# Moving operands of a router's small VectorE operations into PSUM, and an earlier turn of the last x

## The chip, the cores and the metric

The kernel runs on one NeuronCore of one Trainium2 chip. The metric is the device time of one execution in microseconds (us); lower is better. TensorE (PE) does the matrix products and transposes, VectorE (DVE) and ScalarE (ACT) elementwise work and reductions, GpSimd (POOL) elementwise work in SBUF and the indirect transfers, and SyncE (SP) issues most DMA transfers. TensorE writes its results to PSUM, which VectorE and ScalarE can read and write.

## The reference

A hashed attention (4 batches, 8 heads, 768 tokens, 64 wide) feeds a mixture of experts with one expert per token (3072 tokens, 512 wide, 8 experts, hidden width 1024). Cut to what matters:

```python
mask = q_bucket[:, :, :, None] == k_bucket[:, :, None, :]     # six sign bits of q @ proj
scores = np.where(mask, scale * (q @ k.T), -1e9)
attn = exp(scores - max) / (sum + 1e-9)
x = (attn @ v) laid out as (B * S, H * D)
logits = x @ w_gate + modality_bias[modality_id]
e_idx = argmax(logits); gate_w = softmax(logits)[e_idx]
out[e_idx == e] = gate_w * (relu(x @ w1[e]) @ w2[e])          # for each expert e
```

## The kernel before

Attention works on 16 pairs of heads, four pairs to a batch. TensorE's order in attention is written out by hand: for each pair the six strings of `PLAN`, one for each key tile (128 keys), name the steps to take (S: scores, M: the row maxima of the next pair, T: the transposes ("turns"), signs and patterns of the pair after it, A: the product with v, F, f, e, E: one step of `finish` of the batch before, x, y: two steps of `finish_x`, Q: the sum of denominators). A step is what a generator does up to its next `yield`. The other engines' orders are not written by hand: a scheduler fixes them at build time from its own model of the times, in the order of the trace unless an instruction's inputs come late. Each engine runs its queue in order.

GpSimd adds up the exponentials of each pair (L326, tile sp, 128x768, ten additions a pair); in the last pair VectorE takes half of them. `finish(b)` multiplies the gate weights with the unnormalised outputs (L376), turns the products (L385) and the denominators (L392), each copied from PSUM to SBUF by VectorE (L386, L393), inverts the denominators and forms the logits. `route(b)` then takes the best expert of each token, the softmax weight (L618 to L621) and, with a small matrix product of the one-hot choices (L613, L615), the token's place in its expert's list (L624 to L632); GpSimd writes (token, weight) to that place in a table in DRAM (L635). All of these are VectorE operations on 128 partitions by 2 to 104 elements, nearly all with inputs and outputs in SBUF. `finish_x(b)` turns the outputs back to rows (L424), scales them (L426) and writes x to DRAM (L428).

The experts work in blocks of up to 256 tokens of one expert; two early blocks ("e") take tokens of batches 0 to 2 alone, so that they can start while batch 3 is routed. `early_slots` and `late_slots` work out, from the counts per expert, which expert and which rows of the table belong to each block: `above` (L646, L648), `cumulate` (L653 to L657) and `assign` (L664 to L683). SyncE reads expert and row from that result, then loads the block's list (`tb`, L770) and the weights (`raw`, L752, L754, eight transfers of 512 KB per block); GpSimd gathers the rows of x (`xg`, L774). ScalarE casts each weight tile (L760) and VectorE or GpSimd forms its remainder (L762); the same is done to x (`xh`, `xl`, L787). TensorE then does three products for each tile (L797 to L799, L839 to L841).

Two PSUM buffers named `psx` serve the turns, signs, patterns, sums, `finish`, `route` and `finish_x`. In the last pair (i = 15) nothing is computed for a next pair. The early table is traced after attention:

```python
with tc.high_priority(offset=CFG["hpf"]):
    tabs["e"] = early_slots()
```

Of the kernel before, what the change touches and what calls it, by code (L numbers as in the profile page):

```python
# [74 lines left out]
def attention(ctx, actx, tc, a, x_d, l_d, route=None, setup=None):  # L75
# [292 lines left out]
    def finish(b):  # L368

        ts_ = [st[4 * b + c] for c in range(4)]  # L370
        gsb = bp.tile([P, S], F32, name="gsb")
# [19 lines left out]
        for j in range(3):
            nc.tensor.transpose(tp[:, j], gs[:, j * P:(j + 1) * P], ident)  # L392
        nc.vector.tensor_copy(out=gq.rearrange("p j h a c -> p (j h a c)"), in_=tp[:, 0:3].rearrange("p j r -> p (j r)"))  # L393
        yield
        gv = gn.rearrange("p t (h r) -> p t h r", r=16)
        f = bp.tile([P, NT, 8], F32, name="f")
        rin = bp.tile([P, NT, 8], F32, name="rin")
        rv = rin.rearrange("p t (c h) -> p t c h", h=2)
        for h in range(2):
            for half in range(2):  # L400
                ts = slice(3 * half, 3 * half + 3)
                nc.vector.tensor_scalar(out=rv[:, ts, :, h], in0=gq[:, 0:3, h, half, 0:4], scalar1=1e-9, scalar2=None, op0=ALU.add)
        yield
        nc.vector.tensor_scalar(out=f, in0=rin, scalar1=1e-8, scalar2=float(S), op0=ALU.is_lt, op1=ALU.mult)
        nc.vector.tensor_tensor(out=rin, in0=rin, in1=f, op=ALU.add)
        nc.vector.reciprocal(rin, rin)
        fin[b] = (ts_, rin)
        yield
        gl = bp.tile([P, NT, 8, 8], F32, name="gl")
        nc.vector.tensor_tensor(out=gl, in0=gv[:, :, :, 0:8], in1=rin.unsqueeze(3).broadcast_to([P, NT, 8, 8]), op=ALU.mult)  # L410
        yield
        lg = bp.tile([P, NT, 8], F32, name="lg")
        nc.vector.tensor_reduce(out=lg, in_=gl.rearrange("p t h e -> p t e h"), axis=AX.X, op=ALU.add)
        yield
        yield from route(b, lg, ps_x)
# [31 lines left out]
    with tc.manual_schedule(engines={mybir.EngineType.PE}):  # L447
# [19 lines left out]
        for i in range(NPR):  # L467
# [9 lines left out]
            for kt in range(NT):  # L477
                for c in PLAN[kt]:
# [44 lines left out]
E = 8  # L523
# [4 lines left out]
EARLY = CFG["early"]  # L528
NBIG, SURE_BIG = 13, 12 - EARLY
# [16 lines left out]
def router(ctx, tc, a, x_d, tab):  # L546
# [5 lines left out]
    step = const.tile([P, 2, 12], F32, name="kstep")  # L552
# [6 lines left out]
    run = [const.tile([P, E], F32, name=f"run{j}") for j in range(2)]  # L559

    def setup():
        for t, n in ((tok, "c_tok"), (e8, "c_e8"), (step, "c_step"), (slot, "c_slot"), (low, "c_low")):
            nc.sync.dma_start(out=t, in_=a[n])
        with tc.tile_pool(name="rtmp", bufs=1) as tmp:
# [24 lines left out]
            nc.gpsimd.memset(run[0], 0.0)  # L589

    scattered = []

    def route(b, lg, ps):
        l = wk.tile([P, NT, E], F32, name="l")
# [3 lines left out]
        d = wk.tile([P, NT, E], F32, name="rd")  # L598
        nc.vector.tensor_tensor(out=d, in0=l, in1=m.unsqueeze(2).broadcast_to([P, NT, E]), op=ALU.subtract)
        ex = wk.tile([P, NT, E], F32, name="rex")  # L600
        nc.scalar.activation(ex, d, AF.Exp)
        yield
        w = wk.tile([P, NT, E], F32, name="rw")
# [4 lines left out]
        nc.vector.tensor_tensor(out=oh, in0=w, in1=wm.unsqueeze(2).broadcast_to([P, NT, E]), op=ALU.is_equal)  # L608
        yield
        pp = ps.tile([P, HALF], F32, name="psx")  # L610
# [5 lines left out]
        rec = wk.tile([P, NT, 2], I32, name="rec", bufs=2)  # L616
        sm = wk.tile([P, NT], F32, name="rsum")
        nc.vector.tensor_reduce(out=sm, in_=ex, axis=AX.X, op=ALU.add)  # L618
        nc.vector.tensor_scalar(out=sm, in0=sm, scalar1=1e-9, scalar2=None, op0=ALU.add)
        nc.vector.reciprocal(rec[:, :, 1].bitcast(F32), sm)  # L620
        nc.vector.tensor_copy(out=rec[:, :, 0], in_=tok[:, b])  # L621
        yield
        rb = wk.tile([P, E], F32, name="rb")
        nc.vector.tensor_tensor(out=rb, in0=run[b % 2], in1=base, op=ALU.add)  # L624
        rk = wk.tile([P, NT, E], F32, name="rk")
        nc.vector.tensor_tensor(out=rk, in0=pp[:, 0:NT * E].rearrange("p (t e) -> p t e", e=E), in1=rb.unsqueeze(1).broadcast_to([P, NT, E]), op=ALU.add)
        nc.vector.tensor_tensor(out=run[(b + 1) % 2], in0=run[b % 2], in1=pp[:, 64:64 + E], op=ALU.add)
        nc.vector.tensor_tensor(out=rk, in0=rk, in1=oh, op=ALU.mult)
        pos = wk.tile([P, NT], F32, name="pos")
        nc.vector.tensor_reduce(out=pos, in_=rk, axis=AX.X, op=ALU.add)  # L630
# [3 lines left out]
        for t in range(NT):  # L634
            ins = nc.gpsimd.indirect_dma_start(out=tab, out_offset=bass.IndirectOffsetOnAxis(ap=posi[:, t:t + 1], axis=0), in_=rec[:, t], in_offset=None).ins  # L635
# [8 lines left out]
    def above(cnt, row, name):  # L644
        g = wk.tile([P, E, 12], F32, name="sg")
        nc.vector.tensor_tensor(out=g, in0=cnt.unsqueeze(2).broadcast_to([P, E, 12]), in1=step[:, row].unsqueeze(1).broadcast_to([P, E, 12]), op=ALU.is_gt)  # L646
        nb = wk.tile([P, E], F32, name=name)
        nc.vector.tensor_reduce(out=nb, in_=g, axis=AX.X, op=ALU.add)  # L648
        return nb

    def cumulate(nb, name):
        c2 = wk.tile([P, E, E], F32, name="sc2")
        nc.vector.tensor_tensor(out=c2, in0=low, in1=nb.unsqueeze(1).broadcast_to([P, E, E]), op=ALU.mult)  # L653
        cu = wk.tile([P, E], F32, name=name)
        nc.vector.tensor_reduce(out=cu, in_=c2, axis=AX.X, op=ALU.add)
# [332 lines left out]
```

## Time and profile before

| | us |
|---|---|
| median of 3 timed runs (864.04 to 867.50) | 866.99 |
| the profiled execution, its own time | 862.96 |
| its span in the profile | 861.1 |
| TensorE busy in the span | 801.3 |
| VectorE busy | 600.8 |
| ScalarE busy | 498.3 |
| GpSimd busy | 457.2 |

The profile is one execution; its times are counted from the start of the span. A row of the order in time says when a group began, how long it took from its first start to its last end, on which engine, at which line, what it wrote and read, how many instructions were merged, and in brackets how long the engine had been idle and what released it. [...]

### The profile page before, as it was taken

How to read it: one execution, taken by the hardware profiler on the slowest of the kernel's cores; microseconds unless marked ns; L12 is line 12 of the kernel's file. 1: busy time of each engine (PE TensorE's matmuls, PEld its weight loads, DVE VectorE, ACT ScalarE, POOL GpSimd, SP SyncE). 2: the span in 40 equal slices, each digit the busy share in tenths (PEclk: the TensorE clock that was granted, in tenths of full speed). 3: DMA queues.
4: the chain of work that ended last, by engine and by line, in shares of the span. 5: the costliest groups of instructions: out<-in, count | busy, mean ns of one | idle time of the engine just before them, and what ended most of it. 6: DMA issues, size and time to landing. Idle time of an engine off the chain costs nothing.

```text
span 861.1 us, 14524 instructions
## 1 busy us (share of the span) xinstructions
PE 801.3 (93%) x5154; PEld 590.9 (69%) x5154; DVE 600.8 (70%) x1029; ACT 498.3 (58%) x953; POOL 457.2 (53%) x347
## 2 busy tenths in 40 slices
PE   6799999999999999999989787889999999999993
PEld 3466666666667656566746345779999999998992
DVE  6777678797877897776877767766555565567650
ACT  4567676676667566566744343355555555557551
POOL 5377779677887867976667664232222221122110
PEclk9899999999999999999999797999999999999997
DMA  6423212320431132132101254597777767679650
GB/s 173 112 75 92 74 43 68 93 74 19 118 116 63 55 93 74 56 99 68 38 19 31 72 160 147 113 325 222 222 218 232 222 214 234 200 230 299 215 148 22
DMA packets 76753, 110.87 MB, mean 129 GB/s; under 512 B 10495, under 2 KB 52095, under 8 KB 76672
## 3 DMA queue, kind: packets, MB, share of 16 engines
q1 hardware_dynamic: 70880, 95.14, 37.4%
q0 software_dynamic: 4928, 13.14, 4.1%
q10 hardware_dynamic: 864, 1.57, 0.6%
q8 instruction: 43, 0.70, 0.3%
q14 instruction: 38, 0.31, 0.2%
HBM read 84.83 MB, written 13.33 MB: 114 GB/s over the span
## 4 chain that ended last, share of the span: by engine, by line
PE 75%; DVE 10%; issue 6%; DMA 4%; ACT 2%; POOL 1%; SPq 1%; POOLq 0%; DVEq 0%; ACTq 0%
PE psu L341 13%; PE pss L305 8%; PE pss L306 7%; PE psm L239 5%; PE yps L839 5%; PE yps L841 5%; PE yps L840 5%; PE hps L797 4%; PE hps L799 4%; PE hps L798 4%; PE psx L207 3%; PE psx L180 3%; PE psm L245 3%; PE psx L222 2%; PE psx L268 1%
## 5 line engine op out<-in xcount | busy, mean ns | idle before, releaser
L326 POOL TENSOR_TENSOR sp<-sp,pb 128x768 f32<-128x768 f32 x124 | 224.9, 1849 | 38.3 <-ACT pb L323 38.1
L762 DVE TENSOR_TENSOR w<-raw,w 128x1024 fp32r<-128x1024 f32 x108 | 138.9, 1287 | 99.6 <-ACT w L760 93.7
L241 DVE TENSOR_REDUCE mx<-psm 128x1 f32<-128x512 f32 x192 | 131.3, 687 | 41.6 <-PE psm L239 40.4
L760 ACT CAST w<-raw 128x1024 fp32r<-128x1024 f32 x112 | 116.9, 1047 | 69.7 <-PE yps L841 50.7
L341 PE MATMUL psu<-pb,vt 128*64 128x512 f32 (+1 forms) x768 | 137.4, 501 | 0.0
L318 ACT ACTIVATE pb<-pss 128x512 f32<-128x512 f32 x192 | 112.9, 609 | 27.1 <-PE pss L306 18.6
L797 PE MATMUL hps<-xh,w 128*128 128x256 f32 x384 | 109.4, 286 | 2.1 <-DVE hl L804 1.9
L798 PE MATMUL hps<-xl,w 128*128 128x256 f32 x384 | 109.1, 284 | 0.0
L799 PE MATMUL hps<-xh,w 128*128 128x256 f32 x384 | 108.8, 284 | 0.0
L341 PEld LDWEIGHTS psu<-pb,vt 128*64 128x64 f32 x768 | 51.8, 139 | 79.8 <-issue 73.1
L774 POOL DMA_INDIRECT xg<-x_d,tb x26 | 32.7, 1259 | 123.6 <-DMA tb<-tab 115.7
L847 POOL DMA_INDIRECT out<-y,tb x26 | 33.9, 1305 | 117.2 <-ACT y L846 63.9
L839 PE MATMUL yps<-w,hl 128*128 128x512 f32 x208 | 82.9, 398 | 0.9 <-DVE hl L827 0.9
L841 PE MATMUL yps<-w,hh 128*128 128x512 f32 x208 | 81.3, 391 | 0.0
L840 PE MATMUL yps<-w,hh 128*128 128x512 f32 x208 | 81.0, 389 | 0.0
L323 ACT ACTIVATE pb<-pss 128x512 f32<-128x512 f32 x96 | 57.7, 601 | 38.5 <-PE pss L306 36.0
L305 PE MATMUL pss<-m_0g,s_0g 128*128 128x512 f32 x192 | 71.5, 372 | 6.3 <-DVE m_0g L270 3.9
L797 PEld LDWEIGHTS hps<-xh,w 128*128 128x128 f32 x384 | 73.9, 193 | 3.5 <-DVE hl L804 2.6
L798 PEld LDWEIGHTS hps<-xl,w 128*128 128x128 f32 x384 | 73.9, 192 | 1.2 <-issue 0.8
L799 PEld LDWEIGHTS hps<-xh,w 128*128 128x128 f32 x384 | 73.8, 192 | 0.0
L803 ACT ACTIVATE hh<-hps 128x256 fp32r<-128x256 f32 x96 | 36.6, 384 | 64.0 <-PE hps L799 57.9
L305 PE MATMUL pss<-m_1g,s_1g 128*128 128x512 f32 x192 | 69.5, 362 | 1.2 <-ACT pb L323 0.8
(214 smaller groups left out, 1773.3 us busy)
## 6 DMA issues: line engine op xcount, KB each, us to landing
raw<-moe_w SPq DMA_DIRECT2D x112, 512.0 KB
qk<-q SPq DMA_DIRECT2D x32, 192.0 KB
qk<-k SPq DMA_DIRECT2D x32, 192.0 KB
vt<-v SPq DMA_DIRECT2D x16, 384.0 KB
x_d<-xs SPq DMA_DIRECT2D x18, 256.0 KB
m_1g<-m_1g SPq DMA_DIRECT2D x16, 192.0 KB
s_1g<-s_1g SPq DMA_DIRECT2D x16, 192.0 KB
m_0g<-m_0g SPq DMA_DIRECT2D x15, 192.0 KB
```

The costliest lines, as they stand in the source:

```text
L241: nc.vector.tensor_reduce(out=mx[:, qt + j, hi, 0:1], in_=mp, axis=AX.X, op=ALU.max)
L305: nc.tensor.matmul(out, t["s1"][h][:, ks], t["m1"][h][:, cs], start=True, stop=False)
L326: (nc.vector if h and i in CFG["spd"] else nc.gpsimd).tensor_tensor(out=t["sp"][:, h], in0=(t["pb"][0] if kt == 1 else t["sp"])[:, h], in1 ...
L341: nc.tensor.matmul(t["u"][part][64 * h:64 * h + 64, 0:w], t["v"][:, h, kt], t["pb"][kt][:, h, COLS[part]], start=False, stop=(kt == NT - 1 ...
L760: nc.scalar.copy(out=hi, in_=r)
L762: (nc.gpsimd if pool else nc.vector).tensor_tensor(out=lo, in0=r, in1=hi.bitcast(F32), op=ALU.subtract)
L797: nc.tensor.matmul(hps, lo[:, c, fs], xh[:, c], start=(c == 0), stop=False)
L798: nc.tensor.matmul(hps, hi[:, c, fs], xl[:, c], start=False, stop=False)
L799: nc.tensor.matmul(hps, hi[:, c, fs], xh[:, c], start=False, stop=(c == 3))
L839: nc.tensor.matmul(yps[g], hl[fc][:, gs], hi[:, fb], start=(fc == 0), stop=False)
L840: nc.tensor.matmul(yps[g], hh[fc][:, gs], lo[:, fb], start=False, stop=False)
L841: nc.tensor.matmul(yps[g], hh[fc][:, gs], hi[:, fb], start=False, stop=(fc == 7))
```

## The change

Small operations of `finish`, `route`, `early_slots` and, by form alone, `late_slots` are laid out anew. In `finish` the denominators are turned first and inverted from PSUM; the gate products are multiplied straight from PSUM, without the copies gn and gq; the logits and the operands that follow (l, d, w) lie in the unused half of the same psx tile, which `route` is handed. In `route` the places are worked out in the psx tile of the one-hot product, the constant 1e-9 is a ninth column of the exponentials, the running counts are kept a second time with the base added (runb), and the token numbers are written once at the start. `finish` has 13 steps instead of 19. `early_slots` gets a psx tile in which nearly every VectorE operation has one operand; two inputs that would both lie there are copied by ScalarE. It is traced inside attention, at the second key tile of the last pair. `late_slots` has the same code with an area in SBUF. Constants are folded so that `assign` has fewer operations. In the last pair, `finish_x` of batch 2 takes two steps at the start of each of the first three key tiles.

```diff
     def finish(b):
+        gs = gsum[b]
+        tp = ps_x.tile([P, MAIN], F32, name="psx")
+        for j in range(3):
+            nc.tensor.transpose(tp[:, j * P:(j + 1) * P], gs[:, j * P:(j + 1) * P], ident)
+        gq = tp[:, 0:3 * P].rearrange("p (j h a c) -> p j h a c", j=3, h=2, a=2)
+        r = tp[:, 3 * P:3 * P + 8 * NT].rearrange("p (t c) -> p t c", c=8)
...
+        nc.vector.tensor_scalar(out=f, in0=r, scalar1=1e-8, scalar2=float(S), op0=ALU.is_lt, op1=ALU.mult)
+        nc.vector.tensor_tensor(out=rin, in0=r, in1=f, op=ALU.add)
+        nc.vector.reciprocal(rin, rin)
+        yield
...
-            nc.vector.tensor_copy(out=gn[:, 4 * w:4 * w + n], in_=tp[:, 0:n])
...
-        nc.vector.tensor_copy(out=gq.rearrange("p j h a c -> p (j h a c)"), in_=tp[:, 0:3].rearrange("p j r -> p (j r)"))
...
+            nc.vector.tensor_tensor(out=gl[:, 4 * w:4 * w + n], in0=tp[:, 0:n * P].rearrange("p (t h r) -> p t h r", h=8, r=16)[:, :, :, 0:8],
+                                    in1=rin[:, 4 * w:4 * w + n].unsqueeze(3).broadcast_to([P, n, 8, 8]), op=ALU.mult)
+            if w == 0:
+                yield
+        area = tp[:, 2 * P:4 * P]
+        nc.vector.tensor_reduce(out=area[:, 0:48].rearrange("p (t e) -> p t e", e=8), in_=gl.rearrange("p t h e -> p t e h"), axis=AX.X, op=ALU.add)
+        yield from route(b, area, ps_x)
...
             for kt in range(NT):
+                if i == NPR - 1 and kt == 1:
+                    before_last(ps_x.tile([P, MAIN], F32, name="psx"))
+                if i == NPR - 1 and kt < 3:
+                    next(xs, None)
+                    next(xs, None)
...
-    def route(b, lg, ps):
+    def route(b, area, ps):
+        lg, l, d, w = (area[:, 48 * j:48 * j + 48].rearrange("p (t e) -> p t e", e=E) for j in range(4))
...
-        nc.vector.tensor_scalar(out=sm, in0=sm, scalar1=1e-9, scalar2=None, op0=ALU.add)
-        nc.vector.tensor_copy(out=rec[:, :, 0], in_=tok[:, b])
-        nc.vector.tensor_tensor(out=rb, in0=run[b % 2], in1=base, op=ALU.add)
...
+        rk, ro = (pp[:, 128 + 48 * j:176 + 48 * j].rearrange("p (t e) -> p t e", e=E) for j in range(2))
+        pos = pp[:, 256:256 + NT]
...
+    def above(cnt, row, sp, out):
+        cp = sp[:, 0:E]
+        nc.scalar.copy(out=cp, in_=cnt)
...
+        ns = wk.tile([P, E], F32, name="snb")
+        nc.scalar.copy(out=ns, in_=nb)
+        nc.vector.tensor_tensor(out=cx, in0=cu, in1=ns, op=ALU.subtract)
...
-        nc.vector.tensor_scalar(out=r, in0=r, scalar1=float(DUMMY), scalar2=None, op0=ALU.add)
-        nc.vector.tensor_copy(out=out[:, 1], in_=r)
+        nc.vector.tensor_scalar(out=out[:, 1], in0=r, scalar1=float(DUMMY), scalar2=None, op0=ALU.add)
...
+    return route, early_slots, late_slots, setup, lambda: wk.tile([P, 512], F32, name="area")
...
-        with tc.high_priority(offset=CFG["hpf"]):
-            tabs["e"] = early_slots()
+        tabs["e"] = eslot[0]
...
-        tabs["b"], tabs["s"], tot = late_slots()
+        tabs["b"], tabs["s"], tot = late_slots(late_area())
```

## Rows read from the trace of the kernel before

**Rows 1.** The page, engines' busy time, share of the span, instructions.

```profile
PE 801.3 (93%) x5154; PEld 590.9 (69%) x5154; DVE 600.8 (70%) x1029; ACT 498.3 (58%) x953; POOL 457.2 (53%) x347
```

**Rows 2.** Busy time by stretch (stretch, length, busy by engine, granted clock, DMA).

```profile
400.50:434.60 34.10, 30.90 (x210) 19.39 (x209) 28.59 (x59) 20.32 (x43) 25.47 (x19) 1.00 0.18 47
461.30:480.00 18.70, 15.23 (x86) 9.16 (x86) 16.06 (x44) 6.15 (x12) 16.75 (x15) 0.91 0.14 28
480.00:490.00 10.00, 5.84 (x31) 3.91 (x28) 9.47 (x6) 2.30 (x5) 7.41 (x5) 0.84 0.01 0
490.00:500.00 10.00, 7.87 (x34) 3.79 (x32) 2.91 (x4) 6.06 (x12) 2.25 (x1) 0.81 0.91 287
...
517.00:530.00 13.00, 6.74 (x35) 2.89 (x31) 9.91 (x7) 5.38 (x8) 8.54 (x6) 0.66 0.50 156
...
584.50:607.80 23.30, 23.30 (x154) 21.41 (x153) 14.04 (x19) 13.16 (x20) 5.35 (x4) 1.00 0.75 229
```

**Rows 3.** The chain that ended last, 475 to 500 us (start, length, what).

```profile
479.13 8.32 DVE selr L682
...
490.45 6.16 DMA raw<-moe_w
```

**Rows 4.** Order in time, VectorE and GpSimd, 459 to 488 us.

```profile
459.90 3.62 POOL L326 TENSOR_TENSOR sp<-pb,pb 128x768 f32<-128x768 f32 x2 [3.42 <-ACT pb L323]
460.97 0.21 DVE L626 TENSOR_TENSOR rk<-psx,rb 128x48 f32<-128x48 f32 x1
461.21 0.60 DVE L628 TENSOR_TENSOR rk<-rk,oh 128x48 f32<-128x48 f32 x1
463.04 0.50 DVE L632 CAST posi<-pos 128x6 int32<-128x6 f32 x1
473.22 14.19 POOL L326 TENSOR_TENSOR sp<-sp,pb 128x768 f32<-128x768 f32 x8
478.89 0.17 DVE L681 TENSOR_REDUCE selr<-selx 128x2 f32<-128x16 f32 x1
479.10 8.34 DVE L682 TENSOR_SCALAR selr<-selr 128x2 f32<-128x2 f32 x1
```

**Rows 5.** VectorE's groups by line, 100 to 480 us (busy us, mean ns, idle).

```profile
L293 DVE TENSOR_TENSOR vs<-psx,vs 32x64 fp32r<-32x64 f32 x24 | 5.4, 224 | 5.5 <-ACT vs L289 4.5 <-PE pss L306 0.9
L619 DVE TENSOR_SCALAR rsum<-rsum 128x6 f32<-128x6 f32 x3 | 5.3, 1773 | 0.1
L624 DVE TENSOR_TENSOR rb<-run,ke 128x8 f32<-128x8 f32 x3 | 4.6, 1526 | 0.0
L405 DVE TENSOR_TENSOR rin<-rin,f 128x48 f32<-128x48 f32 x3 | 0.6, 209 | 0.1
L626 DVE TENSOR_TENSOR rk<-psx,rb 128x48 f32<-128x48 f32 x3 | 0.6, 208 | 0.2
```

**Rows 6.** Order in time, TensorE, with what ended its waits.

```profile
433.62 0.50 PE L239 MATMUL psm<-s_0g,m_0g 128*128 128x512 f32 x1 [2.67 <-DVE mx L247]
468.17 0.51 PE L245 MATMUL psm<-s_1g,m_1g 128*128 128x256 f32 x2 [1.20 <-DVE mx L241]
488.10 0.55 PE L305 MATMUL pss<-m_0g,s_0g 128*128 128x256 f32 x1 [3.88 <-DVE m_0g L270]
```

**Rows 7.** Order in time, all engines, 505 to 530 us.

```profile
505.25 7.54 POOL L326 TENSOR_TENSOR sp<-sp,pb 128x768 f32<-128x768 f32 x3 [2.63 <-ACT pb L323]
...
517.77 0.99 POOL L774 DMA_INDIRECT xg<-x_d,tb  x1 [1.35 <-DMA x_d<-xs]
519.41 7.53 DVE L762 TENSOR_TENSOR w<-raw,w 128x1024 fp32r<-128x1024 f32 x2 [0.68 <-ACT w L760]
521.30 0.66 PE L785 MATMUL psx<-ident,xg 128*128 128x128 f32 x2 [3.19 <-DMA xg<-x_d,tb]
527.59 2.79 PE L376 MATMUL psx<-ut,gst 128*32 128x512 f32 x16 [2.38 <-DVE xl L787]
```

**Rows 8.** Tile psx, 185 to 225 us: ScalarE's evacuation (ns minimum/median/maximum).

```profile
L184 ACT CAST m_1g<-psx x4: 422/522/618, 188.5 to 218.1; 128x512 fp32r<-128x512 f32 x2, 128x256 fp32r<-128x256 f32 x2
```

More of the change, by code (lines that the diff above doesn't have):

```diff
@@ L398, in finish @@
[L398 to L415, printed above, removed]
+                nc.tensor.transpose(tp[:, j * P:(j + 1) * P], gsb[:, (4 * w + j) * P:(4 * w + j + 1) * P], ident)
@@ L528 @@
 EARLY = CFG["early"]
+NSTEP = N // TS
 NBIG, SURE_BIG = 13, 12 - EARLY
@@ L551, in router @@
     e8 = const.tile([P, 3, E], F32, name="ke8")
-    step = const.tile([P, 2, 12], F32, name="kstep")
+    step = const.tile([P, 2, NSTEP], F32, name="kstep")
     slot = const.tile([P, 16], F32, name="kslot")
@@ L559, in router @@
     run = [const.tile([P, E], F32, name=f"run{j}") for j in range(2)]
+    runb = [const.tile([P, E], F32, name=f"runb{j}") for j in range(2)]
+    rec = const.tile([P, B, NT, 2], I32, name="rec")
+    ex = const.tile([P, NT, E + 1], F32, name="rex")
+    wbase = const.tile([P, E], F32, name="wbase")
     def setup():
@@ L608, in route @@
         nc.vector.tensor_tensor(out=oh, in0=w, in1=wm.unsqueeze(2).broadcast_to([P, NT, E]), op=ALU.is_equal)
+        sm = wk.tile([P, NT], F32, name="rsum")
+        nc.vector.tensor_reduce(out=sm, in_=ex, axis=AX.X, op=ALU.add)
+        nc.vector.reciprocal(rec[:, b, :, 1].bitcast(F32), sm)
         yield
-        pp = ps.tile([P, HALF], F32, name="psx")
+        pp = ps.tile([P, 512], F32, name="psx")
         for j in range(NT):
@@ L683, in assign @@
[L683 to L694 removed]
+            w = cx
@@ new lines, in assign, with early_slots @@
+        nc.vector.tensor_scalar(out=out[:, 1], in0=r, scalar1=float(DUMMY), scalar2=None, op0=ALU.add)
+    def early_slots(sp):
+        out = const.tile([P, 2, EARLY], I32, name="eslot")
+        nb, cu, cx, r = (sp[:, 8 * j:8 * j + 8] for j in range(1, 5))
+        above(run[(B - 1) % 2], 0, sp, nb)
+        cumulate(nb, cu, cx)
+        es = wk.tile([P, E], F32, name="es")
+        nc.vector.tensor_scalar(out=es, in0=cx, scalar1=-1.0, scalar2=float(EARLY), op0=ALU.mult, op1=ALU.add)
+        nc.vector.scalar_tensor_tensor(out=early, in0=es, scalar=0.0, in1=nb, op0=ALU.max, op1=ALU.min)
+        assign(EARLY, cu, cx, wbase, TS, out, sp[:, 64:64 + EARLY * E], r[:, 0:EARLY])
@@ L701, in late_slots @@
         cnt = run[B % 2]
-        fb = above(cnt, 1, "fb")
-        nb = wk.tile([P, E], F32, name="lnb")
-        nc.vector.tensor_tensor(out=nb, in0=fb, in1=early, op=ALU.subtract)
-        cu, cx = cumulate(nb, "lcu")
-        assign(NBIG, cu, cx, early, TS, big)
-        sb = wk.tile([P, E], F32, name="sb")
-        nc.vector.scalar_tensor_tensor(out=sb, in0=fb, scalar=float(TS), in1=cnt, op0=ALU.mult, op1=ALU.is_lt)
-        su, sx = cumulate(sb, "lsu")
-        assign(NSML, su, sx, fb, 0, sml)
+        fbp, nb, cu, cx = (sp[:, 8 * j:8 * j + 8] for j in range(1, 5))
@@ L711, in late_slots @@
+        r = sp[:, 40:56]
+        above(cnt, 1, sp, fbp)
+        nc.vector.tensor_tensor(out=nb, in0=fbp, in1=early, op=ALU.subtract)
+        cumulate(nb, cu, cx)
         nc.vector.tensor_copy(out=tot[:, 0:1], in_=cu[:, E - 1:E])
-        nc.vector.tensor_copy(out=tot[:, 1:2], in_=su[:, E - 1:E])
         over = wk.tile([P, 2], F32, name="over")
         nc.vector.tensor_scalar(out=over[:, 0:1], in0=cu[:, E - 1:E], scalar1=SURE_BIG + 0.5, scalar2=None, op0=ALU.is_gt)
+        wb = wk.tile([P, E], F32, name="wb")
@@ new lines, in late_slots @@
+        eb = wk.tile([P, E], F32, name="eb")
+        nc.vector.scalar_tensor_tensor(out=eb, in0=early, scalar=float(TS), in1=wbase, op0=ALU.mult, op1=ALU.add)
+        nc.vector.scalar_tensor_tensor(out=wb, in0=fbp, scalar=float(TS), in1=wbase, op0=ALU.mult, op1=ALU.add)
+        assign(NBIG, cu, cx, eb, TS, big, sp[:, 128:128 + NBIG * E], r[:, 0:NBIG])
+        sb = sp[:, 64:72]
+        nc.vector.scalar_tensor_tensor(out=sb, in0=fbp, scalar=float(TS), in1=cnt, op0=ALU.mult, op1=ALU.is_lt)
+        su, sx = sp[:, 72:80], sp[:, 80:88]
```

116 lines of the change are left out of this document (44 added, 72 removed).

## The prediction

> **What bounds the kernel now.** I read the page first: TensorE is busy 93% of the span, VectorE 70% [rows 1]. A share says nothing of stages, so the busy time by stretch comes next [rows 2], each stretch a pair of heads or a step of the hand-over to the experts. The reader is to see two regimes. From 584.5 us on TensorE is full, 23.30 of 23.30 us for one block of 256 tokens, and stays so until the last blocks: whatever reaches that point earlier moves the end by as much. Before it lies the loss: 3.2 us idle in 400.5 to 434.6, 3.5 in 461.3 to 480, then 4.2 in 480 to 490, 2.1 in 490 to 500 and 6.3 in 517 to 530, with the granted clock at 0.91, 0.84, 0.81 and 0.66 in the last four. Then I read the chain of work that ended last, 479 to 498 us [rows 3]: it runs 8.32 us through one VectorE instruction at L682, goes to the slot loads, and then through a 6.16 us weight transfer.
>
> The order in time says why [rows 4]. L682 adds a constant to 128x2 values and takes 8.34 us. It starts inside GpSimd's run of eight denominator additions, 473.22 to 487.41, and ends as that run ends. At 461 us, inside another such run, L626 (one input in PSUM) takes 0.21 us and L628 (both in SBUF, same 128x48) 0.60; the conversion L632 (SBUF to SBUF) 0.50 for six values. Over the three routed batches the same split holds [rows 5]: L619 1773 ns and L624 1526, while L626 stays at 208 and L293, a PSUM input too, at 224. L405 (two SBUF inputs) shows the plain price, 209. So an elementwise VectorE instruction that lives wholly in SBUF waits for GpSimd; with an operand in PSUM it does not.
>
> **The change, term by term** (time on the path to 584.5).
>
> A, routing of batches 0 to 2. L619 and L624 lose their place, L608, L621, L628 and L632 get a PSUM operand or go. VectorE loses in waiting 3 x (1.77 - 0.17) + 3 x (1.53 - 0.17), about 9 us, with 0.17 us as the plain price of so small an operation (L681 [rows 4]), and some more at the others. Nearly all lies beside TensorE's own work: of TensorE's waits in these stretches only one follows a blocked chain, 2.67 us at 433.62 [rows 6], where the next maximum stood behind L619 and L621. I take 2.7 back; bounds 0 and 4.
>
> B, the table of early slots. Most of its operations ran ahead of maxima that pair 14 computes for pair 15; TensorE waited 1.20 us for one of these at 468.17 [rows 6]. They go to the last pair, which computes no maxima. 1.2; bounds 0 and the whole idle time of 461.3 to 480, 3.5.
>
> C, L682 itself. Its successor reads PSUM, so of 8.34 us about 0.16 remains: 8.2. Behind it on VectorE stood m_0g, for which TensorE waited 3.88 us [rows 6], and SyncE's load of the slot. The stretch 480 to 490 has no other owner. Bounds 4.2 (TensorE's own idle time there) and 8.3.
>
> D, the weight transfer in the chain [rows 3]. A cast that waits for its weights stands in ScalarE's queue ahead of the exponentials. The table came 8.2 us late to an order that was fixed at build time; in time, the wait should shrink. But the table is now traced at the second key tile of the last pair, and attention ends sooner, so some stays. TensorE's loss in 490 to 500 is 2.1 idle and 7.87 x 0.19 = 1.5 at the low clock. I take 2.0; bounds 0 and 6.2.
>
> F, the start of the experts. The last pair's x (three transposes, multiplies and SyncE writes) moves from its third, fifth and sixth key tile to its first three. SyncE's queue is moved past too: two of the writes should now stand before the weight loads, which follow the slot table. Before, the gather left at 517.77, released by x's last write, and landed after TensorE had waited 3.19 us [rows 7]. Those writes now land some ten us before attention ends. What then remains is the split of weights: two VectorE adds of L762 took 7.53 us beside GpSimd's own L762, and xl and TensorE's 2.38 us at 527.59 stand behind them [rows 7]. These adds are not changed. Of 517 to 530, 13 us, the work at full clock is 6.74 x 0.66 = 4.4, so 8.6 is lost; I take 4.0 for the gather, its idle time and a little clock; bounds 0 and 8.6.
>
> G, 530 to 584.5. The last batch's routing runs beside block 0; GpSimd does transfers there and a single weight split, so little was blocked. TensorE's small gaps stay. The late table keeps its operands in SBUF (its area comes from an SBUF pool) and gets three ScalarE copies, which hide behind blocks 0 and 1, since block 2 is the first to use it. If they don't, block 2's gather is late by a few us. 0; bounds -5 and 3.
>
> H, what is added. The logits, and the first steps of routing, live in one of the two psx buffers, so that turns, signs and x of the next steps have one; the early table (18 VectorE operations where there were 23, and two ScalarE copies, at most 0.5 us each by L184's [rows 8]) holds one for about 18 x 0.17 + 2 x 0.5 = 4.1 us. Two turns in a row then wait for an evacuation, 0.52 us [rows 8], once a batch and once in the last pair: -2.1. If four turns a batch wait 1 us each it is -12 and -4.1 more: bounds 0 and -16. Writing PSUM from VectorE is not in the trace: reading it costs nothing (L626 against L405), and the farthest row, L293, is 15 ns above; at most 26 instructions a batch make 0.4 us, off the path. That one I take as nothing. The copies into gn and gq that go lay beside TensorE's work: nothing, too.
>
> Sum: 2.7 + 1.2 + 8.2 + 2.0 + 4.0 - 2.1 = 16.0 us. The profiled execution took 862.96 us (span 861.1 and 1.9 around it); that gives 847. The three timed runs have a median of 866.99, 4.0 above the profiled one. The same gain from it gives **851 us**.
>
> [...]
>
> **Rivals.** (1) The forecast. (2) ScalarE's wait for weights stays: the casts stand before exponentials that are now sooner. For it speaks the 6.16 us in the chain; against it, that the lateness came from L682. D is not had, and one more such transfer is paid: 851 + 2 + 6 = 859.
>
> (3) Slower: the wait finds another instruction. L762 and the last pair's own L326 on VectorE still have two SBUF inputs. If the order now puts two weight splits into a long run of GpSimd in the last pair, VectorE stands for up to 14.2 us each (the run of eight [rows 4]), with m_0g, xs and the early table behind it. It decides from 20.3 us of such time (16.0 + 4.3); two full runs, 28.4 us, give 851 + 28 = 879. Against it: in the last pair VectorE takes half of the additions, and the longest run there was 7.54 us [rows 7].
> [...]
>
> (4) A PSUM operand, an output above all, puts a fixed term on each small operation. If it were a third of L405's 0.21 us, (3 x 26 + 18) x 0.07 = 6.7 us, half of it on the path, it gives 854. L626 speaks against it for inputs, nothing for outputs. [...]
>
> (5) The change does not do what it says: an output in PSUM does not free the instruction, and L682's successor waits as long. Then B, F and H remain, 3.1 us: 864. L626 and L293 speak against it, though both write SBUF.
>
> **How the numbers follow.** Chances: 0.62, 0.19, 0.08, 0.05, 0.06 in this order. The forecast's own range is 842 to 859: below, D and F at their full bounds (4.2 and 4.6 more); above, C at its lower bound, nothing of D and half of F (4.0, 2.0 and 2.0 less). The range for all is 839 to 864: at its low end A and B are had in full too (1.3 and 2.3), at its high end stands rival 5; left out above are rival 3 and the worst of H. About 0.5%, 4.3 us, is what a measurement of this kernel can tell from no change. Faster than 862.7: forecast, rivals 2 and 4, so 0.86. Rival 5 is the same, 0.06. Slower 0.08.
>
> **What would show it.** No VectorE instruction of the router or table above 0.4 us while GpSimd adds; the successor of L682 at 0.16 to 0.2 us; no TensorE gap of 2 us near L613 and the maxima (A, B); the last pair shorter by 8 us or more, with the granted clock near 1.0 (C); the gather's issue before the last additions of GpSimd (F); the first full stretch of TensorE starting near 568 us instead of 584.5. The prediction is wrong if ScalarE's cast waits again for weights inside the last pair (2), if L762 on VectorE is long there (3), if small PSUM operations take 0.27 us instead of 0.21 (4), or if turns wait for psx (H).

## The result and the profile after

The changed kernel takes 856.6 us (median of 4 runs, 854.1 to 860.46) where the kernel before takes 867.25 beside it: ratio 0.989, 95% interval 0.984 to 0.994, so 1.1% faster, inside the range and 5.6 us above the 851 forecast. Five more rounds gave 856.19 us and 0.992 (0.988 to 0.995). The execution that was profiled took 860.46 us, its span 858.6. The us of a kernel are the median of all its timed runs but one, a run of route_only of 1541.35 us; the ratios leave out runs of a slower state of the chip.

The table cuts the span at events that every kernel here has. A pair starts at its first `psu <- lone` product (L336 in the changed kernel); the first and the fourth turn are the first L785 product of block 0 and of block 3. All entries are us, read from the order in time.

| kernel | start of pair 0 | pairs 0 to 14 | pair 5 | pair 9 | 14 to 15 | 15 to first turn | first to fourth turn | rest |
|---|---|---|---|---|---|---|---|---|
| before | 47.5 | 413.8 | 28.6 | 28.6 | 38.3 | 21.7 | 78.5 | 261.3 |
| changed | 50.2 | 419.2 | 35.1 | 29.4 | 27.0 | 24.5 | 76.9 | 260.8 |
| changed, again | 47.3 | 425.6 | 35.5 | 35.2 | 28.6 | 19.6 | 72.6 | 260.8 |

The step from pair 14 to 15 is 11.3 us shorter (B, C and D together: 11.4 forecast). Ahead of it the kernel lost 5.4 us, in the second profile 11.8, where A and H together had promised a gain of 0.6. In the second profile pair 0 starts no later than before; in the first the granted clock, as a share of the full one, was 0.53 from 38 to 45 us, ahead of it.

The table does not hold the whole gain. The two profiled executions of its first rows are 2.5 us apart, the medians 10.7: the profile of the kernel before is shorter than its four timed runs, that of the changed kernel is the longest of its four. Where the rest of the gain lies no profile shows. One candidate, not shown, is a wait that the old order meets in some executions: c_alone, below, met one of 7.06 us that the profile before does not have.

First VectorE's groups by line in the changed kernel, 100 to 480 us, to be held against [rows 5] (busy us, mean ns, idle):

```profile
L166 DVE TENSOR_TENSOR n<-qk,n 128x384 fp32r<-128x384 f32 x22 | 35.3, 1607 | 4.0 <-POOL sp L326 2.8 <-issue 0.6
L625 DVE TENSOR_TENSOR psx<-psx,runb 128x48 f32<-128x48 f32 x3 | 0.6, 215 | 0.4
L628 DVE TENSOR_TENSOR psx<-psx,oh 128x48 f32<-128x48 f32 x3 | 0.6, 205 | 0.0
L631 DVE CAST posi<-psx 128x6 int32<-128x6 f32 x3 | 0.5, 155 | 0.0
```

The same view of the kernel before, a line not shown yet:

```profile
L166 DVE TENSOR_TENSOR n<-qk,n 128x384 fp32r<-128x384 f32 x22 | 18.7, 849 | 3.4 <-POOL sp L326 1.7 <-issue 1.1
```

The small operations do what the change says: L628, input and output in PSUM, takes 205 ns, L625 215, the conversion 155. But L166, a subtraction with two SBUF inputs that the diff does not touch, has 16.6 us more than before, in the same 22 instructions. 7.0 of them are in a single instruction of pair 5. The rest is in instructions of 2.1 to 2.7 us where the kernel before has 0.5 to 2.2, and TensorE waited for none of these: its only wait of over 2 us between 100 and 460 us is the one that follows.

Order in time of pair 5, changed kernel (GpSimd, VectorE, TensorE; in brackets the wait and what ended it):

```profile
199.75 1.16 POOL L634 DMA_INDIRECT tab<-rec,posi  x1 [0.17 <-DVE gs L364]
...
207.27 14.42 POOL L326 TENSOR_TENSOR sp<-sp,pb 128x768 f32<-128x768 f32 x8
221.65 0.99 POOL L166 TENSOR_TENSOR n<-qk,n 128x384 fp32r<-128x384 f32 x1
222.61 0.99 POOL L277 TENSOR_TENSOR va<-vt 128x384 f32<-128x384 f32 x1
223.56 3.56 POOL L326 TENSOR_TENSOR sp<-pb,pb 128x768 f32<-128x768 f32 x2
219.95 7.60 DVE L166 TENSOR_TENSOR n<-qk,n 128x384 fp32r<-128x384 f32 x1
228.20 0.80 PE L239 MATMUL psm<-s_0g,m_0g 128*128 128x512 f32 x1 [6.15 <-DVE mx L247]
```

The six scatters (L634) now come before the run of eight additions; in the kernel before they came a pair later, at 225 us. The same pair there, order in time:

```profile
198.78 14.39 POOL L326 TENSOR_TENSOR sp<-sp,pb 128x768 f32<-128x768 f32 x8 [2.53 <-ACT pb L323]
216.92 0.56 DVE L166 TENSOR_TENSOR n<-qk,n 128x384 fp32r<-128x384 f32 x1
217.40 1.02 POOL L166 TENSOR_TENSOR n<-qk,n 128x384 fp32r<-128x384 f32 x1 [4.22 <-ACT n L162]
225.44 1.17 POOL L635 DMA_INDIRECT tab<-rec,posi  x1 [0.17 <-issue]
```

So the run now starts 13.0 us after the pair began instead of 7.6, and VectorE's L166, which starts 25.7 us into the pair in both kernels, falls into its end. Here it stayed 7.60 us, behind everything that GpSimd did back to back, to 227 us. VectorE's maximum stands behind it, and TensorE waits 6.15 us for that.

The early table in its new place, order in time of VectorE and GpSimd, against [rows 4]:

```profile
488.27 0.26 DVE L647 TENSOR_TENSOR sg<-psx,kstep 128x96 f32<-128x96 f32 x1 [1.02 <-ACT psx L645]
488.86 0.23 DVE L652 TENSOR_TENSOR sc<-psx,klow 128x64 f32<-128x64 f32 x1
493.70 0.16 DVE L679 TENSOR_SCALAR eslot<-psx 128x2 int32<-128x2 f32 x1
486.17 3.61 POOL L326 TENSOR_TENSOR sp<-sp,pb 128x768 f32<-128x768 f32 x2 [0.21 <-ACT pb L323]
495.88 1.86 POOL L326 TENSOR_TENSOR sp<-pb,pb 128x768 f32<-128x768 f32 x1 [6.10 <-ACT pb L323]
```

L682's successor, L679, takes 0.16 us. But GpSimd is idle from 489.8 to 495.9, so most of the table had nothing to wait for, wherever its operands lie.

The busy time by stretch (length, busy of TensorE, its weight loads, VectorE, ScalarE, GpSimd, granted clock, DMA), against [rows 2]:

```profile
469.40:496.40 27.00, 24.73 (x152) 15.94 (x151) 18.44 (x48) 11.77 (x26) 19.18 (x14) 1.00 0.14 49
504.00:521.00 17.00, 11.44 (x57) 4.53 (x57) 15.08 (x4) 6.21 (x11) 14.42 (x7) 0.94 0.46 140
560.00:582.00 22.00, 17.78 (x103) 16.41 (x102) 13.21 (x18) 11.66 (x19) 6.87 (x6) 0.84 0.88 276
582.00:605.30 23.30, 23.30 (x153) 21.40 (x152) 14.04 (x18) 13.17 (x21) 5.56 (x4) 1.00 0.76 227
```

From 469 to 496 us TensorE is busy 24.73 of 27.00 us at full clock. The next loss is 504 to 521, with only four VectorE instructions in 15.08 us. Two of them, a run of GpSimd's beside them and the product that waited, in the order in time (from 504.41 to 508.57 GpSimd adds and splits a weight):

```profile
508.53 7.05 POOL L326 TENSOR_TENSOR sp<-sp,pb 128x768 f32<-128x768 f32 x3
504.23 6.93 DVE L326 TENSOR_TENSOR sp<-sp,pb 128x768 f32<-128x768 f32 x1 [0.67 <-ACT pb L323]
511.08 2.84 DVE L762 TENSOR_TENSOR w<-raw,w 128x1024 fp32r<-128x1024 f32 x1
519.47 1.49 PE L361 MATMUL psx<-sp,ones 128*32 128x384 f32 x4 [2.99 <-DVE sp L326]
```

### The profile page after: what moved, and what is told of

Same layout as the page of the kernel before. It is cut to its first block, busy times and chain, and to the rows that moved or that the text cites. A ratio compares the mean times of both kernels' runs of the same rounds, so it can differ in the third digit from the quotient of the medians.

```text
span 858.6 us, 14509 instructions
## 1 busy us (share of the span) xinstructions
PE 802.3 (93%) x5154; PEld 593.7 (69%) x5154; DVE 592.6 (69%) x1001; ACT 499.8 (58%) x958; POOL 460.3 (54%) x351
## 4 chain that ended last, share of the span: by engine, by line
PE 79%; DVE 7%; ACT 4%; issue 4%; DMA 3%; POOL 1%; SPq 0%; POOLq 0%; ACTq 0%; DVEq 0%
PE psu L341 13%; PE pss L305 8%; PE pss L306 7%; PE hps L798 5%; PE hps L797 5%; PE hps L799 5%; PE psm L239 5%; PE yps L839 5%; PE yps L841 5%; PE yps L840 5%; PE psx L180 3%; PE psx L207 3%; PE psm L245 3%; DMA x_d<-xs 2%; DVE n L166 2%
## 5 line engine op out<-in xcount | busy, mean ns | idle before, releaser
L326 POOL TENSOR_TENSOR sp<-sp,pb 128x768 f32<-128x768 f32 x124 | 225.3, 1856 | 36.9 <-ACT pb L323 36.6
L762 DVE TENSOR_TENSOR w<-raw,w 128x1024 fp32r<-128x1024 f32 x108 | 135.0, 1252 | 95.0 <-ACT w L760 94.4
L341 PE MATMUL psu<-pb,vt 128*64 128x512 f32 (+1 forms) x768 | 135.5, 495 | 0.0
L247 DVE TENSOR_REDUCE mx<-psm 128x2 f32<-128x512 f32 x96 | 66.1, 689 | 7.8 <-PE psm L245 4.4
```

What stands on the lines that cost most here:

```text
L326: (nc.vector if h and i in CFG["spd"] else nc.gpsimd).tensor_tensor(out=t["sp"][:, h], in0=(t["pb"][0] if kt == 1 else t["sp"])[:, h], in1 ...
L341: nc.tensor.matmul(t["u"][part][64 * h:64 * h + 64, 0:w], t["v"][:, h, kt], t["pb"][kt][:, h, COLS[part]], start=False, stop=(kt == NT - 1 ...
L762: (nc.gpsimd if pool else nc.vector).tensor_tensor(out=lo, in0=r, in1=hi.bitcast(F32), op=ALU.subtract)
```

## The experiments

Each kernel was timed beside the kernel before on the same chip, and the ratio is to those runs. The rows come from three chips, so they are to be compared by the ratio first. Stages are cut as above, in one profile of each kernel.

| kernel | us | ratio (95%) | 0 to 14 | pair 5 | pair 9 | 14 to 15 | 15 to first turn | first to fourth |
|---|---|---|---|---|---|---|---|---|
| after_again | 856.19 | 0.992 (0.988 to 0.995) | 425.6 | 35.5 | 35.2 | 28.6 | 19.6 | 72.6 |
| early_sbuf | 857.27 | 0.994 (0.990 to 0.998) | 423.9 | 35.1 | 34.8 | 25.5 | 22.7 | 72.2 |
| areas_sbuf | 856.92 | 0.993 (0.989 to 0.997) | 426.0 | 35.0 | 34.9 | 25.5 | 22.8 | 73.0 |
| c_alone | 859.07 | 0.994 (0.990 to 0.998) | 420.3 | 28.6 | 28.6 | 31.5 | 22.7 | 74.4 |
| route_late5 | 849.73 | 0.983 (0.980 to 0.985) | 410.7 | 28.6 | 28.6 | 28.9 | 26.0 | 73.3 |
| route_only | 850.6 | 0.985 (0.982 to 0.987) | 419.5 | 35.1 | 29.4 | 24.9 | 21.9 | 72.8 |
| x_late | 852.85 | 0.988 (0.986 to 0.991) | 418.1 | 35.1 | 29.4 | 24.4 | 23.9 | 75.9 |
| adds_vector | 851.15 | 0.985 (0.983 to 0.988) | 419.8 | 35.1 | 29.3 | 27.0 | 18.3 | 72.6 |
| split_gpsimd | 842.90 | 0.973 (0.967 to 0.978) | 408.4 | 28.3 | 28.1 | 28.6 | 19.6 | 71.5 |
| late_vector | 849.61 | 0.976 (0.968 to 0.984) | 414.2 | 28.6 | 28.6 | 28.6 | 19.8 | 73.2 |
| split_vector_x | 838.29 | 0.968 (0.963 to 0.974) | 407.9 | 28.2 | 28.1 | 24.9 | 21.8 | 70.2 |
| split_vector_early | 835.80 | 0.964 (0.960 to 0.969) | 408.1 | 28.1 | 28.2 | 25.4 | 17.4 | 73.6 |

**after_again**, no edit.

> The changed kernel once more, for the terms of single stages. Theory: what follows from the written order recurs, so VectorE's L166 of pair 5 again waits 5 to 8 us behind GpSimd's run, VectorE's xs (L419) again waits 3 to 5 us for the x_d writes beside block 0, and the two L326 of the last pair on VectorE again take 5 us or more; the later start of pair 0 (2.7 us, granted clock 0.54 before it) does not recur, since no instruction there changed. Time 856 us, 853 to 860. Rival: L166's wait comes from the moment at which this one run met it; then pair 5 takes 28 to 30 us instead of 35.1, and the run is near 850.

Pair 5's wait came again (L166 7.97 us); xs's two waits were shorter (1.73 and 3.60 us instead of 2.95 and 5.44), and so were the last pair's (L326 2.58, L762 3.38). Pair 9 is the surprise, 35.2 us instead of 29.4 with the same instructions in the same order on every engine. First the changed kernel, then this run, order in time:

```profile
333.90 14.36 POOL L326 TENSOR_TENSOR sp<-sp,pb 128x768 f32<-128x768 f32 x8
348.55 1.02 POOL L166 TENSOR_TENSOR n<-qk,n 128x384 fp32r<-128x384 f32 x1 [0.28 <-ACT n L162]
348.07 0.61 DVE L166 TENSOR_TENSOR n<-qk,n 128x384 fp32r<-128x384 f32 x1
```

```profile
332.08 14.38 POOL L326 TENSOR_TENSOR sp<-sp,pb 128x768 f32<-128x768 f32 x8
346.43 0.99 POOL L166 TENSOR_TENSOR n<-qk,n 128x384 fp32r<-128x384 f32 x1
344.66 7.65 DVE L166 TENSOR_TENSOR n<-qk,n 128x384 fp32r<-128x384 f32 x1
```

Where GpSimd paused for 0.28 us at the end of its run, L166 slipped through in 0.61 us; where it went straight on, it took 7.65. The other kernels with this order agree: in the three more where pair 9 took 29.3 to 29.4 us GpSimd paused 0.17 to 0.21 us and L166 took 0.68 to 0.72, in the two more where it took 34.8 and 34.9 there was no pause and L166 took 7.14 and 7.40. L166 also started later in the four short pairs, 26.9 us into the pair instead of 25.7 to 25.8; which of the two let it through is not separated. Pair 9 is thus a coin toss of some 6 us; this run lost it and still ended 4.1 us sooner, by its start of pair 0, its last pair and its turns.

**early_sbuf and areas_sbuf**: the operands back in SBUF, the order of instructions almost kept.

```diff
-    def early_slots(sp):
-        out = const.tile([P, 2, EARLY], I32, name="eslot")
+    def early_slots(sp0):
+        out, sp = const.tile([P, 2, EARLY], I32, name="eslot"), wk.tile([P, 128], F32, name="earea")
...
-        above(run[(B - 1) % 2], 0, sp, nb)
+        above(run[(B - 1) % 2], 0, sp0, nb)
```

areas_sbuf has that and

```diff
-        r = tp[:, 3 * P:3 * P + 8 * NT].rearrange("p (t c) -> p t c", c=8)
+        r = bp.tile([P, NT, 8], F32, name="rr")
...
-        area = tp[:, 2 * P:4 * P]
+        area = bp.tile([P, 2 * P], F32, name="area")
...
-        rk, ro = (pp[:, 128 + 48 * j:176 + 48 * j].rearrange("p (t e) -> p t e", e=E) for j in range(2))
-        pos = pp[:, 256:256 + NT]
+        rk, ro = (wk.tile([P, NT, E], F32, name=f"rk{j}") for j in range(2))
+        pos = wk.tile([P, NT], F32, name="pos")
```

> The changed kernel with the early table's area in SBUF behind its first operation (the order of VectorE's instructions hardly changes, the table stays in the last pair). Theory of the prediction (the operand in PSUM frees the instruction, term C): the table's small operations wait again wherever GpSimd adds; GpSimd stood idle for most of this stretch, so 1 to 4 us are lost of the 8 to 11 won. Rival (it was the new place that freed the table, at a moment when GpSimd has nothing to do): no change, within 1 us, and no operation of the table above 0.4 us. If the operand alone had done it, all of 8 us would be lost again.

> The same, and the areas of finish and route in SBUF too (r, logits, l, d, w, rk, ro, pos). Theory: elementwise operations between them wait 1 to 8 us each inside GpSimd's runs, in the profile at L611, L613, L617, L628 or L631, and what they cost on the path is term A, 2 to 4 us more than early_sbuf. Rival: the order alone did it, or TensorE's own work hides these waits; then the time is that of early_sbuf within 1.5 us, though the waits show in VectorE's rows.

Both rivals hold in time. In early_sbuf one operation of the table waited all the same (L652, 1.03 us instead of 0.23, beside an addition of GpSimd). In areas_sbuf the waits do come back, in VectorE's groups by line, 100 to 480 us:

```profile
L628 DVE TENSOR_TENSOR rk<-rk,oh 128x48 f32<-128x48 f32 x3 | 3.9, 1295 | 0.0
L384 DVE TENSOR_TENSOR rin<-rr,f 128x48 f32<-128x48 f32 x3 | 3.9, 1294 | 0.0
```

L628 goes from 205 to 1295 ns and L384 from 198 to 1294 with little changed but where the operands lie (GpSimd's order is the same, VectorE's almost), and with GpSimd adding beside all three L628 and all three L384 of the changed kernel; so the operand did free these instructions. But pairs 0 to 14 take 426.0 us against 425.6: the freed time lay beside TensorE's work. With the order almost kept, the placement itself is worth nothing measurable; what moved the time is the order.

**c_alone**: one edit of the kernel before.

```diff
-        nc.vector.tensor_scalar(out=r, in0=r, scalar1=float(DUMMY), scalar2=None, op0=ALU.add)
-        nc.vector.tensor_copy(out=out[:, 1], in_=r)
+        if n == EARLY: nc.scalar.activation(out[:, 1], r, AF.Copy, bias=float(DUMMY)); return
+        nc.vector.tensor_scalar(out=r, in0=r, scalar1=float(DUMMY), scalar2=None, op0=ALU.add); nc.vector.tensor_copy(out=out[:, 1], in_=r)
```

> The kernel before with one edit: ScalarE adds the constant and converts, in place of VectorE's L682 and L683; every other VectorE instruction keeps its place. Theory (terms C and D): VectorE's 8.3 us are gone, m_0g and the slot load come 8 us sooner, the granted clock of 480 to 500 us goes back to 1.0: 867 - 8 - 2 = 857 us, as fast as the whole change. Rival: ScalarE's queue or the weights become the bound in the last pair at once, so that only TensorE's own 4.2 us in 480 to 490 us come back: 863 us.

Pairs 14 to 15 shorten by 6.8 us: term C is real. First to fourth turn shortens by 4.1, but that is no more than the two profiles of the changed kernel differ by there (4.3). The rest of the step is the rival's, order in time of ScalarE and TensorE:

```profile
485.08 0.20 ACT L682 ACTIVATE eslot<-selr 128x2 int32<-128x2 f32 x1 [1.28 <-DVE selr L681]
495.17 1.04 ACT L760 CAST w<-raw 128x1024 fp32r<-128x1024 f32 x1 [4.45 <-DMA raw<-moe_w]
498.58 0.79 PE L305 MATMUL pss<-m_0g,s_0g 128*128 128x512 f32 x1 [4.67 <-ACT pb L318]
```

The cast still waits 4.45 us for its weights ahead of the exponentials, and TensorE waits 4.67 us. The profiled run also met an L166 of 7.06 us in pair 10, which took 35.7 us: the old order can meet that wait too.

**route_late5**: the counting products five steps later in batches 0 to 2, so the scatters return to their old place.

```diff
-        pp = ps.tile([P, 512], F32, name="psx")
+        yield from [None] * (5 if b < B - 1 else 0); pp = ps.tile([P, 512], F32, name="psx")
```

> The changed kernel with five steps more between the one-hot and the counting products of batches 0 to 2, so that GpSimd's six scatters stand again behind VectorE's L166, where they stood in the kernel before; nothing else moves. Theory: the routing part gives back some 12 us, because the scatters come a pair sooner, start GpSimd's run of eight additions 5 us later, and VectorE's L166 then meets that run; with the scatters back, pairs 5 and 9 take 28 to 29 us instead of 35, no L166 lasts above 3 us, and the kernel takes 856 - 12 = 844 us, 842 to 848. Rival: L166's long wait belongs to VectorE's own new order (fewer small operations ahead of it, so it starts sooner); then it stays and the time is 854 to 858.

Pairs 5 and 9 take 28.6 us; no L166 lasts above 2.64. In pair 5, order in time, GpSimd and VectorE:

```profile
198.93 14.39 POOL L326 TENSOR_TENSOR sp<-sp,pb 128x768 f32<-128x768 f32 x8 [1.89 <-ACT pb L323]
217.52 1.01 POOL L166 TENSOR_TENSOR n<-qk,n 128x384 fp32r<-128x384 f32 x1 [4.20 <-ACT n L162]
217.04 0.56 DVE L166 TENSOR_TENSOR n<-qk,n 128x384 fp32r<-128x384 f32 x1
```

Pairs 0 to 14 take 410.7 us, 3.1 less than before: this is term A as it was meant (2.7). The kernel is at 849.7, not 844; in part, by this profile, for its 26.0 us from pair 15 to the first turn.

**route_only**: the routing part alone.

```diff
-                    before_last(ps_x.tile([P, MAIN], F32, name="psx"))
-                if i == NPR - 1 and kt < 3:
+                    pass
+                if i == NPR - 1 and kt < 0:
...
-        tabs["e"] = eslot[0]
+        with tc.high_priority(offset=CFG["hpf"]): tabs["e"] = early_slots(late_area())
```

> The routing part of the change alone: new finish and route with their operands in PSUM, but the early table behind the attention in an SBUF area, and the last pair's x in its old steps. Prediction's terms A and H alone: -2.7 + 2.1, so 865 to 867 us. Theory now: from pair 0 to pair 14 it takes 12 us more than the kernel before (L166 behind GpSimd's run in pairs 5 and 9). If the table's operations now meet the run of additions in pair 14, as L682 did, the time is 866 + 12 = 878 us; if the sooner routing lets them pass ahead of it, 866 + 12 - 8 = 870 us.

At 850.6 us it is better than every figure expected and not slower than the whole change. The table lies wholly in SBUF here. It runs in pair 13, order in time:

```profile
440.47 0.99 POOL L634 DMA_INDIRECT tab<-rec,posi  x1 [0.27 <-DVE area L662]
...
447.82 14.36 POOL L326 TENSOR_TENSOR sp<-sp,pb 128x768 f32<-128x768 f32 x8
440.65 0.17 DVE L665 TENSOR_TENSOR area<-area,selx 128x16 f32<-128x16 f32 x1
442.05 0.16 DVE L679 TENSOR_SCALAR eslot<-area 128x2 int32<-128x2 f32 x1
```

Routing ends sooner, so the table is done at 442.2 us, ahead of the run of additions; the scatters between did not hold VectorE (L665 0.17 us, L679 0.16). That alone removes L682's stall; neither the table's new place nor the earlier x is needed for it.

**x_late**: the changed kernel with x in its old steps.

```diff
-                if i == NPR - 1 and kt < 3:
+                if i == NPR - 1 and kt < 0:
```

> The changed kernel with the last pair's x in its old steps (third, fifth and sixth key tile). Prediction's term F gives the earlier x 4.0 us: 860 us, the gather again behind x's last write, TensorE waiting some 3 us for it after attention. Rival: the last additions of the denominators, not the gather, hold TensorE there, so moving x back costs less than 1 us: 856.

852.85 us and 0.988, against 0.989 and 0.992 for the changed kernel: moving x back cost nothing that shows. TensorE does wait for the gather again, 3.7 us ahead of the first turn, but the step from pair 14 to 15 is 2.6 and 4.2 us shorter than in the two profiles of the changed kernel.

**adds_vector**: the last pair's additions on VectorE.

```diff
-                    (nc.vector if h and i in CFG["spd"] else nc.gpsimd).tensor_tensor(out=t["sp"][:, h], in0=(t["pb"][0] if kt == 1 else t["sp"])[:, h], in1=pb[:, h], op=ALU.add)
+                    (nc.vector if i in CFG["spd"] else nc.gpsimd).tensor_tensor(out=t["sp"][:, h], in0=(t["pb"][0] if kt == 1 else t["sp"])[:, h], in1=pb[:, h], op=ALU.add)
```

> The changed kernel with all ten denominator additions of the last pair on VectorE (GpSimd keeps only weight splits and gathers there). Theory: the long L326 and L762 of that stretch (up to 6.9 and 7.5 us where plain ones take 0.96 and 1.22) wait for GpSimd; without GpSimd's additions each takes about its plain time, ten additions are 10 us on VectorE, and attention's end comes 1 to 4 us sooner: 853 to 855 us. Rival: VectorE's own queue becomes the bound of the last pair, no gain or a loss of 2 us.

Pair 15 to the first turn takes 18.3 us, the shortest of any kernel so far; two additions in a row take 1.81 us and L762 1.21 and 1.23.

**split_gpsimd**: four of VectorE's L166 to GpSimd (rq lists the head pairs whose L166 are all GpSimd's).

```diff
-CFG = dict(... rq=(1, 2), ...)
+CFG = dict(... rq=(1, 2, 9, 13), ...)
```

> The changed kernel with four of VectorE's L166 moved to GpSimd, those of the weigh steps of pairs 5 and 9 (two head pairs, 9 and 13, split on GpSimd alone, as two others are already); scatters and all else keep their place. Theory: the long wait in pairs 5 and 9 is that of one instruction with two SBUF inputs inside GpSimd's run; with it gone from VectorE, VectorE's maxima go on, both pairs take 28 to 30 us, 6 to 7 us are won in pair 5 and 0 or 6 in pair 9: 847 to 850 us. Rival: the scatters hold GpSimd itself late, and the pair waits for GpSimd's part whoever does L166: 854 to 857 us.

842.9 us. TensorE's waits of 100 to 460 us (us, times, longest), first after_again, then this kernel:

```profile
PE psm L239 <- DVE mx L247: 12.8, 2, 6.5
```

```profile
PE psx L207 <- DVE bits L209: 1.0, 3, 0.4
PE psx L286 <- ACT s_1g L224: 0.9, 3, 0.5
```

The waiting instruction gone from VectorE, the wait is gone, with the scatters where the change put them. Pairs 0 to 14 take 408.4 us, 5.4 less than in the kernel before.

**late_vector**: route_late5 and adds_vector together.

> The changed kernel with the later scatters of route_late5 and the denominator additions of the last pair on VectorE, as in adds_vector. Theory: the two gains lie in different stretches (pairs 5 and 9; the last pair) and add: 849.7 - 4 = 846 us, with p15 to the first turn of the experts 18 to 19 us where route_late5 had 25.9. Rival: the last pair's gain only moves to the next wait (weights): 849 us.

Pair 15 to the first turn is 19.8 us as expected, but in this profile pair 6 took 35.7 us (L166 6.97): the delay moves the place at which L166 may meet a run and does not rule it out. At 849.61 us, 0.976, the intervals don't tell it from route_late5.

**split_vector_x**: route_only, split_gpsimd and adds_vector together.

> The routing part alone (route_only: table in SBUF ahead of the last pair, x in its old steps) with the L166 of split_gpsimd and the additions of adds_vector. Theory: neither the table's new place nor the earlier x is needed; the wait of pair 5 (35.1 us) goes and the last pair shortens: 851 - 6.5 - 2 = 842.5 us, 840 to 846. Rival: the gather, behind x's last write, now holds the start of the experts by its 3 to 4 us: 846 to 849.

838.29 us. TensorE waits 3.62 us for the gather at the first turn, as the rival said, and the rest is better than expected.

**split_vector_early**: the same with x in its first three steps.

> split_vector_x with the last pair's x back in its first three steps: term F by itself, with the other waits out of the way. Prediction: 4.0 us for the earlier gather; in split_vector_x TensorE waits 3.6 us for the gather after attention, so 838.3 - 3.6 = 834.7 us, the turn of the gathered rows within 2 us of attention's last product (4.4 there). Rival: the earlier multiplies and products only lengthen the last pair by as much (split_vector_x took 24.9 us from pair 14 to 15, kernels with x early 27 to 28.6): 837 to 840.

835.80 us. The wait for the gather is gone and 15 to first turn falls from 21.8 to 17.4, but first to fourth turn grows from 70.2 to 73.6: in the stage rows 1.0 us remains. The two medians differ by 2.5 us and the intervals of the ratios overlap, so what the earlier x is worth stays open. This is the fastest kernel of the study, 3.6% under the kernel before.

## Why the prediction was right, and where it was not

The forecast stood on one mechanism, that an elementwise VectorE instruction wholly in SBUF waits for GpSimd and one with an operand in PSUM does not. areas_sbuf shows it directly for L628 and L384 (1.29 us each there, 0.21 and 0.20 with an operand in PSUM), but it also shows that the gain did not come from it: with the operands back in SBUF and the order almost kept the time stays. The sign and the range held. That the sum came within 5.6 us is in part luck: A missed by 8 us and more, the gain of F is not to be seen, and 4 to 8 us of the timed gain stand in neither profile. In the profiles the fourth turn comes 1.9 and 6.1 us sooner, not 16.

- **A** failed. The 2.7 us are there (route_late5, 3.1; pair 12 to 13 takes 31.8 us instead of 34.1). But the step costed VectorE's instructions and left out that routing that ends sooner issues its six scatters sooner, on GpSimd. They push the run of eight additions into L166's way: 6.4 to 6.9 us in pair 5 in every profile of the order that the change writes, and some 6 more in pair 9 in three of the seven.
- **H** was right in size and wrong in place. It put 2.1 us on held psx buffers, a quarter each to three batches and the last pair. TensorE's waits ahead of products into psx from 100 to 460 us sum to 2.2 us in the changed kernel and to 2.8 in the kernel before. In the last pair, though, two transposes of the earlier x waited 0.56 and 1.42 us until VectorE had read a psx tile, in both profiles; x_late and route_only have neither wait. The second, order in time of TensorE:

```profile
490.12 0.63 PE L417 MATMUL psx<-ident,ut 128*128 128x128 f32 x4 [1.42 <-DVE vs L293]
```

- **B, C, D** gave 11.3 us in the first profile and 9.7 in the second, against 11.4. The agreement is closer than the terms: the earlier x now lies in the same step, and without it (x_late) the step gives 13.9. C by itself is 6.8 us in its step (c_alone), and that kernel's ratio is 0.994. D was right for the changed kernel, where the cast waits 2.64 us ahead of 499.9 us and TensorE is still busy 6.69 of the 7.60 us from 496.4 to 504; with C alone (c_alone) the wait for weights stays, as rival 2 had it. The reason for C was half right: L682 was freed because the table no longer meets a run, not because its operands moved (early_sbuf, route_only).
- **F** was given to the earlier gather. The wait for the gather is gone from the changed kernel, but TensorE waits for the last additions in its place (1.60 and 2.99 us, in the second profile 1.3), and x_late loses nothing. From pair 15 to the fourth turn the kernel before has 100.2 us, the changed kernel 101.4 in one profile and 92.2 in the other; with x in its old steps x_late has 99.8, route_only 94.7 and split_vector_x 92.0. Two profiles of one kernel differ by more than F, so what shortens these turns, and whether C does, is not shown.
- **G** was taken as 0. In the first profile VectorE's xs waited for its own writes beside block 0, order in time:

```profile
557.03 0.69 DVE L419 TENSOR_TENSOR xs<-psx,rin 128x512 f32<-128x512 f32 x1 [5.44 <-DMA x_d<-xs]
```

  The chain of work that ended last runs from there to TensorE, which waited 4.22 us for VectorE's hl at 564.84: the whole idle time of the 560 to 582 stretch above. In the second profile xs waited 3.60 us, TensorE 2.4, and the same turns took 4.3 us less in all; in the kernel before xs waited 3.17 and TensorE 1.7. So the loss is not new, and it swings from run to run.
- **Rivals.** Rival 3 is what took the gain away, at another instruction than the two it named, and before pair 14. L762 and L326 were long too, as it said (2.84 and 6.93 us), which was worth 1.3 to 6.2 us (adds_vector's 18.3 us from pair 15 to the first turn, against 19.6 to 24.5). The length of a wait was no fixed one: at 14.19 / 8 = 1.77 us for one addition L682 sat through nearly five [rows 4], and in pair 5 of the changed kernel L166 sat through the rest of one and four more of GpSimd's instructions, 7.60 us. Elsewhere in the kernel before it was less: L628 took 0.60 us inside a run that went on [rows 4], and the 1.77 and 1.53 us of L619 and L624 [rows 5] are about one addition. The full run of 14.2 us that rival 3 priced is in no profile: the longest waits are those of L682, 8.34 us, and L166, 7.97. Rival 4 falls: L628 takes 205 ns with output in PSUM, L405 took 209 [rows 5], and L625 takes 215 where L626 took 208. Rival 5 falls with areas_sbuf: L384 took 1294 ns with both inputs in SBUF and 198 in the changed kernel with one in PSUM.

## What to carry to other kernels

When a step is made to end sooner, list what it issues on every engine and what that pushes back: six DMA issues on GpSimd cost 6.5 to 12 us here, where the change's routing part won 3. A wait of one engine for another was better taken away here by moving the instruction that waits (split_gpsimd, 842.9 us) than by moving the run it meets (late_vector, where it met the next one). And where a change both moves work and changes its operands, test the two apart before naming the cause.

## What the runs showed of the hardware

Elementwise VectorE instructions with all operands in SBUF waited here for GpSimd's elementwise work, and L166 waited through a whole chain of back-to-back instructions: it took 7.60 us in pair 5 of the changed kernel and 7.97 and 7.65 in after_again; the shortest L166 of the changed kernel took 0.55. Not every wait was so long. In the kernel before, L624 got in behind the first of two additions (order in time):

```profile
219.33 3.63 POOL L326 TENSOR_TENSOR sp<-pb,pb 128x768 f32<-128x768 f32 x2
219.42 1.80 DVE L624 TENSOR_TENSOR rb<-run,ke 128x8 f32<-128x8 f32 x1
```

What decided between the two stays open; pauses of GpSimd of 0.17 to 0.28 us went with the short L166 of pair 9. GpSimd's issue of the scatters did not hold VectorE: in route_only the SBUF operations between them took 0.16 to 0.17 us. Two profiles of one kernel, the same instructions in the same order, differ by 5.8 us in pair 9 (29.4 and 35.2 us), and the second shows a stall, L166's 7.65 us, that the first does not have (0.61).
